# Depth-first stage targets for the planner, taps summed on TensorE, shuffles over alternate partition halves, and weight loads behind the shuffles, in a one-core long convolution with a token MLP

## The chip, the cores and the metric

The kernel runs on one core of a Trainium2 chip. The metric is device time in microseconds, the median of several executions. A core has TensorE (matmuls, results to the PSUM memory of eight banks), VectorE and ScalarE (called DVE and ACT in the profile; both can read PSUM), GpSimd (POOL) and SyncE (SP, which here only issues DMAs). Each engine takes its own instructions strictly in the order in which they stand in its queue.

## The reference, cut to what matters

S = 2048 tokens, D = 448 channels, F = 1792.

```python
def _A_ref(q, k, v, shift_k, ssm_k, ssm_D):
    k_pad = jnp.pad(k, ((0, 0), (ks - 1, 0), (0, 0)))
    k_shift = jnp.zeros_like(k)
    for t in range(ks):                                   # ks = 4 taps
        k_shift = k_shift + k_pad[:, t:t + S, :] * shift_k[:, ks - 1 - t][None, None, :]
    kv = k_shift * v
    ...
    y_f = kv_f * kf_f[None, :, :, :]                      # Fourier transforms of kv and ssm_k, length 2S
    y = irfft2(y_f)[:S]
    y = y + kv * ssm_D[None, None, :]
    return q * y

def _B_ref(x, w1, b1, w2, b2):
    h = _layernorm(x, axis=-1)
    u = jnp.einsum("bsd,sf->bdf", h, w1) + b1
    u = _gelu(u)
    y = jnp.einsum("bdf,fs->bds", u, w2) + b2
    return y.transpose(0, 2, 1)

h = x + _A_ref(_layernorm(x), A_k, A_v, ...)
out = h + _B_ref(_layernorm(h), ...)
```

## The kernel before, in words

A sequence of 2048 is held as 128 partitions of R = 16 consecutive tokens (index r). The convolution is a Fourier transform in two steps of matmuls. **Stage 1** (`emit_stage1`, L863 and L865) multiplies, for each r, the slice by a cosine and a sine table into a pair of PSUM banks; ACT or VectorE evicts the pair (128 x 896, L870) into one of eight buffers (`wring`); GpSimd issues a DMA, the *shuffle* (L873), which spreads the buffer's 128 rows over eight partitions of a tile `T`, sixteen rows each. It runs once for the filter ("k", transposed before by 64 small matmuls in `emit_kT`, L848) and once for kv ("u"). **Stage 2** (`emit_stage2`, L887, evictions L639 to L643) needs all sixteen shuffles of its signal, and gives the spectrum in sixteen slices j of four matmuls. `emit_products_i1` multiplies the two spectra (L916 and L921, VectorE, two products a slice into a ring `mring` of four) and goes back by eight matmuls a slice (L927); the slice is evicted and shuffled again (L933, the *z shuffles*, into `TZ`). `emit_i2` needs all sixteen z shuffles: for each r it sums in one PSUM bank kv times ssm_D (by an identity matmul, L991) and two table matmuls (L993, L995); VectorE multiplies by normalized q (L998) and adds x (L1001), ACT takes mean and square sums (L1004, L1007), GpSimd the power (L1015, L1018), VectorE normalizes (L1023). `emit_mlp` follows: W1 in two parts (W1A, six of the fourteen column blocks, L1057; W1B, eight, L1065), gelu on ACT (L1048), W2 (L1074), and the last addition and store (L1077, L1081).

`emit_kv` makes kv: for each r VectorE multiplies four shifted rows by the four taps (L829, 128 x 1792), for each two r adds them in two steps (L832, L835) and multiplies by v (L838). It uses two buffers T by turns. `emit_ct` reorders the tables on GpSimd (L897) and transposes them (L903). `emit_tables` makes the tables, among them seven block-diagonal ones (`BD`, L751).

The order of each engine's queue is not written by hand. `_Sched.schedule` is a list scheduler that runs at build time: an operation has a planned duration, and among the ready ones an engine takes that of highest priority, the longest planned path to the end plus a `boost`. So slices of equal rank go side by side. Operations given as `FX` may go to ACT or VectorE, whichever the planner finds free. All weight loads are issued from ACT's queue (`WQ = "act"`), and the memory of W1B and W2 is that of the spectra and `TU`, so their issues wait for the last readers of these. Loads of the inputs are issued by SP.

## Time and profile before

| | us |
|---|---|
| median of 3 executions | 250.05 (248.65 to 251.76) |
| the profiled execution | 249.59 |
| its span, first to last instruction | 247.8 |
| TensorE busy | 190.3 (77%) |
| VectorE busy | 130.1 (53%) |
| ACT busy | 105.4 (43%) |
| GpSimd busy | 51.6 (21%) |
| mean granted TensorE clock | 0.900 |

Times in the profile run from the span's start. PE is TensorE, PEld its weight load. "Busy" rows of groups give the sum and the mean of one in ns, then the idle time of the engine just ahead of them and what ended it. The *chain* follows the instruction that ended last backwards, at each step to what it had waited for. The granted clock is 1.00 or 0.50 in this trace, and a matmul of 448 columns takes correspondingly less or more.

### The profile page before, as it was taken

Reading aid. Unit: us, or ns where it says so; the run is one execution under the profiler, and the core shown is the slowest. Engines: PE = TensorE matmul, PEld = TensorE weight load, DVE = VectorE, ACT = ScalarE, POOL = GpSimd, SP = SyncE. Lnnn points to the kernel's source line nnn. Section 1 sums busy time; section 2 is a strip of 40 time slices with the busy share of each in tenths; the row PEclk is TensorE's granted clock in tenths of the full one; section 3 lists DMA queues with packets and bytes.
Section 4 is the critical chain, followed back from the end, with each engine's and each line's share of the span. In section 5 each row is a group of like instructions: output and inputs, shape, how many; then the busy total and the mean of one; then the engine's idle time right before and its main releaser. Section 6 shows DMA issues by size and latency. Waiting matters only on the chain.

```text
span 247.8 us, 2495 instructions
## 1 busy us (share of the span) xinstructions
PE 190.3 (77%) x913; PEld 95.2 (38%) x913; DVE 130.1 (53%) x253; ACT 105.4 (43%) x164; POOL 51.6 (21%) x97
## 2 busy tenths in 40 slices
PE   0375847795959998787380691999999999999992
PEld 0270101132335434333130240455444566777771
DVE  8999999519984999856110499531000000040225
ACT  5759956784643772535110159980222322100000
POOL 3310744535630014423030003430000000000000
PEclk9996775559997999999987599899999999999998
DMA  5999799999970001489999299100000000001023
GB/s 185 282 369 434 215 201 203 192 241 253 240 217 7 0 0 30 122 222 268 233 366 322 65 352 405 79 1 0 3 0 0 0 0 3 0 33 43 2 109 111
DMA packets 15126, 35.97 MB, mean 145 GB/s; under 512 B 3787, under 2 KB 7499, under 8 KB 14986
## 3 DMA queue, kind: packets, MB, share of 16 engines
q0 software_dynamic: 5376, 11.04, 19.5%
q10 hardware_dynamic: 6016, 14.68, 18.9%
q1 hardware_dynamic: 3722, 10.10, 11.5%
q8 instruction: 7, 0.11, 0.2%
q14 instruction: 5, 0.04, 0.1%
HBM read 22.94 MB, written 1.84 MB: 100 GB/s over the span
## 4 chain that ended last, share of the span: by engine, by line
PE 53%; DMA 21%; DVE 11%; ACT 6%; POOL 3%; issue 3%; SPq 1%; DVEq 0%; ACTq 0%; POOLq 0%
DMA arena<-arena 18%; PE ps L1074 17%; PE ps L1065 10%; PE ps L1057 8%; PE ps L887 7%; PE ps L927 7%; ACT arena L639 5%; DMA arena<-in_A_ssm_k_dram 4%; DVE arena L998 3%; POOL arena L873 2%; PE ps L848 2%; DVE arena L1001 2%; DVE arena L954 1%; DVE arena L1077 1%; ACT arena L870 1%
## 5 line engine op out<-in xcount | busy, mean ns | idle before, releaser
L1074 PE MATMUL ps<-arena 128*128 128x448 bf16 x224 | 45.6, 355 | 0.0
L1077 DVE SCALAR_TENSOR_TENSOR arena<-ps,arena 128x448 bf16<-128x448 f32 x16 | 9.7, 676 | 67.4 <-PE ps L1074 67.4
L1074 PEld LDWEIGHTS ps<-arena 128*128 128x128 bf16 x224 | 31.5, 145 | 13.4 <-ACT arena L1048 3.1
L887 PE MATMUL ps<-arena 128*128 128x448 bf16 x128 | 31.2, 386 | 6.8 <-DMA arena<-arena 2.9
L639 ACT CAST arena<-ps 128x896 bf16<-128x896 f32 (+1 forms) x24 | 20.4, 876 | 33.1 <-PE ps L927 18.1
L927 PE MATMUL ps<-arena 128*128 128x448 bf16 x128 | 27.0, 366 | 9.0 <-ACT arena L639 9.0
L1065 PE MATMUL ps<-arena 128*128 128x448 bf16 x128 | 29.4, 353 | 0.0
L870 ACT CAST arena<-ps 128x896 bf16<-128x896 f32 x30 | 25.5, 940 | 6.3 <-DMA arena<-arena 6.3
L1057 PE MATMUL ps<-arena 128*128 128x448 bf16 x96 | 22.6, 372 | 5.2 <-DVE arena L1023 5.2
L1048 ACT ACTIVATE arena<-ps,arena 128x448 bf16<-128x448 f32 x14 | 8.9, 634 | 38.7 <-PE ps L1057 19.4
L873 POOL DMA_DIRECT2D arena<-arena x32 | 19.5, 608 | 25.6 <-ACT arena L870 19.8
L863 PE MATMUL ps<-arena 128*128 128x448 bf16 x32 | 15.1, 471 | 12.3 <-ACT arena L870 7.8
L927 PEld LDWEIGHTS ps<-arena 128*128 128x128 f16 x128 | 12.2, 101 | 23.9 <-ACT arena L639 12.9
L887 PEld LDWEIGHTS ps<-arena 128*128 128x128 f16 x128 | 11.7, 105 | 23.7 <-issue 6.2
L642 DVE CAST arena<-ps 128x896 bf16<-128x896 f32 x9 | 9.6, 1089 | 14.7 <-PE ps L927 9.6
L1065 PEld LDWEIGHTS ps<-arena 128*128 128x128 bf16 x128 | 12.0, 98 | 12.6 <-ACT arena L1048 2.4
L829 DVE TENSOR_TENSOR arena<-arena 128x1792 bf16<-128x1792 bf16 x16 | 16.4, 1079 | 0.0
L1004 ACT ACTIVATE arena<-arena 128x448 bf16<-128x448 bf16 x16 | 9.2, 576 | 15.6 <-PE ps L993 15.2
L1057 PEld LDWEIGHTS ps<-arena 128*128 128x128 bf16 x96 | 9.8, 103 | 15.0 <-DVE arena L1023 5.5
L865 PE MATMUL ps<-arena 128*128 128x448 bf16 x32 | 15.5, 485 | 0.0
L863 PEld LDWEIGHTS ps<-arena 128*128 128x128 f16 x32 | 3.3, 102 | 30.2 <-ACT arena L870 22.9
L998 DVE TENSOR_TENSOR arena<-ps,arena 128x448 bf16<-128x448 f32 x16 | 9.3, 614 | 10.3 <-PE ps L995 10.1
(75 smaller groups left out, 219.0 us busy)
## 6 DMA issues: line engine op xcount, KB each, us to landing
arena<-arena POOLq DMA_DIRECT2D x48, 224.0 KB, 8.3
arena<-in_B_w_dram ACTq DMA_DIRECT2D x5, 2048.0 KB, 12.9
arena<-in_B_w_dram ACTq DMA_DIRECT2D x2, 1536.0 KB, 23.1
arena<-in_A_ssm_k_dram SPq DMA_DIRECT2D x4, 448.0 KB, 7.6
arena<-in_A_k_dram SPq DMA_DIRECT2D x4, 448.0 KB, 12.0
arena<-in_A_v_dram SPq DMA_DIRECT2D x4, 448.0 KB, 12.6
arena<-in_A_q_dram SPq DMA_DIRECT2D x1, 1792.0 KB, 18.1
out_dram<-arena SPq DMA_DIRECT2D x7, 224.0 KB, 1.9
```

Of the source, the lines that this page charges most:

```text
L639: return e.copy(out=dst(), in_=src())
L829: op("dve", lambda e, W, T=T, i=i, r=r: e.tensor_tensor(out=T[:, i], in0=KH[:, r:r + 4, :], in1=WT, op=ALU.mult), r=[(o_KH + r * DB, 4 * D ...
L863: op("pe", lambda e, W, b=b, r=r: e.matmul(Pb(b, 0), Ct[:, r, :], src[:, r, :], start=True, stop=True), r=[r_C(r), (o_src + r * DB, DB)], ...
L865: op("pe", lambda e, W, b=b, r=r: e.matmul(Pb(b, 1), St[:, r, :], src[:, r, :], start=True, stop=True), r=[r_S(r), (o_src + r * DB, DB)], ...
L870: return e.copy(out=dst, in_=Ppair(b)) if W == "act" else e.tensor_copy(out=dst, in_=Ppair(b))
L873: op(SHQ[r % 2], lambda e, W, w=w, p0=p0: e.dma_start(T[p0:p0 + 29:4].rearrange("p j c d -> p j (c d)"), WR(w.slots[0]).rearrange("p c d - ...
L887: op("pe", lambda e, W, b=b, bi=bi, tab=tab, ci=ci, st=st, sp=sp, j=j: e.matmul(Pb(b, bi), tab, T[:, j, ci, :], start=st, stop=sp), r=rr, ...
L927: i = op("pe", lambda e, W, b=b, bi=bi, tab=tab, mi=mi, m=m, k=k: e.matmul(Pb(b, bi), tab, MR(m.slots[0])[:, mi, :], start=(k % 4 == 0), s ...
L998: op("dve", lambda e, W, b=b, r=r: e.tensor_tensor(out=V[:, r, :], in0=Pb(b), in1=Q[:, r, :], op=ALU.mult), r=[(o_Q + r * DB, DB)], w=[(o_ ...
L1057: op("pe", lambda e, W, r=r, fc=fc, b=bs[fc]: e.matmul(Pb(b), W1A[:, r, 128 * fc:128 * fc + 128], Q[:, r, :], start=(r == 0), stop=(r == R ...
L1065: op("pe", lambda e, W, r=r, fc=fc, b=b: e.matmul(Pb(b), W1B[:, r, 128 * (fc - n0):128 * (fc - n0) + 128], Q[:, r, :], start=(r == 0), sto ...
L1074: op("pe", lambda e, W, r=r, fc=fc, b=b: e.matmul(Pb(b), W2[:, fc, r:S:R], G[:, fc, :], start=(fc == 0), stop=(fc == NFC - 1)), r=[(o_W2 + ...
```

## The change

Parts of it move instructions, others replace them.

- **Priorities.** `boost` gives way to `t0`, a target time in us for each operation: a lower target goes first, and the longest path only breaks ties. The targets rise with r, c or j inside a stage, so one slice is finished before the next is begun. Planned durations of VectorE and of DMA issues change, VectorE takes an `FX` operation only when ACT has a backlog of six or is busy for 0.6 us more, and the planner's model of the shuffles puts successive ones on alternate halves of the DMA engines.
- **Taps.** The two additions of `emit_kv` go; for each r four identity matmuls sum the four products in a PSUM bank, and VectorE multiplies the bank by v (128 x 448, sixteen times).
- **kT** is evicted in eight pieces of two r instead of four pieces of four.
- **Shuffles** write other partitions: shuffle r begins at partition 64·(r mod 2) + 32·(r/2 mod 2) + r/4, so successive ones lie in alternate halves of the 128 partitions. The tables (`pc`, `cp`) are permuted to match; GpSimd's four table copies become eight of half the size.
- **i2** adds the identity matmul last instead of first.
- **Weights** are issued by SP; W1A waits for the last u shuffle, W1B and W2 for the last z shuffle. W2 is cut 4, 3, 4, 3 instead of 4, 4, 4, 2.
- The ssm_k loads go ahead of the shift_k load.

```diff
@@ the planner @@
         for o in ops:
-            prio[o.id] += o.boost
+            prio[o.id] = prio[o.id] * 1e-6 - o.t0
...
+                        if (e == "dve" and len(ops[oid].engs) > 1 and
+                                free_at["act"] - t < self.flex_slack and not self.backlog(ready, ops, started, ready_t, t)):
+                            tmp.append((pr, oid))
+                            continue
...
+                        if o.keng == 8:
+                            rr8 ^= 8
+                            use = range(rr8, rr8 + 8)
@@ the targets (two of three lines) @@
+        T_KV, T_DKV, T_KT, T_K1, T_DK1, T_U1, T_DU1 = 12.0, 3.6, 10.0, 14.0, 1.2, 16.0, 2.0
+        T_K2, T_U2, T_D2, T_CT, T_BIAS, T_I1, T_DI1 = 38.0, 56.0, 1.0, 45.0, 50.0, 60.0, 1.6
@@ emit_kv @@
-                op("dve", lambda e, W, T=T: e.tensor_tensor(out=T[:, :, 0:2, :], in0=T[:, :, 0:2, :],
-                                                            in1=T[:, :, 2:4, :], op=ALU.add),
-                   r=[(o, 8 * DB)], w=[(o, 8 * DB)], n=4 * D)
-                op("dve", lambda e, W, T=T: e.tensor_tensor(out=T[:, :, 0, :], in0=T[:, :, 0, :], in1=T[:, :, 1, :],
-                                                            op=ALU.add),
-                   r=[(o, 8 * DB)], w=[(o, 8 * DB)], n=2 * D)
-                op("dve", lambda e, W, T=T, c=c: e.tensor_tensor(out=V[:, 2 * c:2 * c + 2, :], in0=T[:, :, 0, :],
-                                                                 in1=V[:, 2 * c:2 * c + 2, :], op=ALU.mult),
...
+                for i in range(2):
+                    r = 2 * c + i
+                    b = _Buf(psum)
+                    for j in range(4):
+                        op("pe", lambda e, W, b=b, T=T, i=i, j=j: e.matmul(Pb(b), ID, T[:, i, j, :], start=(j == 0),
+                                                                           stop=(j == 3)),
+                           r=[(o_ID, 256), (o + (i * 4 + j) * DB, DB)], bw=[b], n=D)
+                    op("dve", lambda e, W, b=b, r=r: e.tensor_tensor(out=V[:, r, :], in0=Pb(b), in1=V[:, r, :],
+                                                                     op=ALU.mult),
@@ emit_stage1, and the same for the z shuffles with j @@
+                sch.t0 = T_K1 + T_DK1 * r if tag == "k" else T_U1 + T_DU1 * r
...
-                p0 = 32 * (r >> 2) + (r & 3)
-                op(SHQ[r % 2], lambda e, W, w=w, p0=p0: e.dma_start(
+                p0 = 64 * (r & 1) + 32 * ((r >> 1) & 1) + (r >> 2)
+                shuf[tag] = op(SHQ[r % 2], lambda e, W, w=w, p0=p0: e.dma_start(
@@ emit_i2 @@
-                    op("pe", lambda e, W, b=b, r=r: e.matmul(Pb(b), ID, V[:, r, :], start=True, stop=False),
...
+                    k = op("pe", lambda e, W, b=b, r=r: e.matmul(Pb(b), ID, V[:, r, :], start=False, stop=True),
@@ weights @@
-        WQ = "act"
+        WQ = "sp"
...
-                       w=[(o_W1A + 8 * h * 1536, 8 * 1536)], dmab=128 * 8 * 1536)
+                       w=[(o_W1A + 8 * h * 1536, 8 * 1536)], dmab=128 * 8 * 1536, after=[shuf["u"]])
...
-                       w=[(o_W1B + 8 * h * 2048, 8 * 2048)], dmab=128 * 8 * 2048)
+                       w=[(o_W1B + 8 * h * 2048, 8 * 2048)], dmab=128 * 8 * 2048, after=[shuf["z"]])
```

Three places show how the queues change. First TensorE where the inverse stage runs. Before, L927 are its matmuls, eight a slice, and the rows are two slices twice; `csem_act` and `csem_dve` are waits for ACT and VectorE.

```order
L927 MATMUL ps<-arena 128x448 [waits csem_act]
L927 MATMUL ps<-arena 128x448 x4
L927 MATMUL ps<-arena 128x448 [waits csem_act]
L927 MATMUL ps<-arena 128x448 x10
L927 MATMUL ps<-arena 128x448 [waits csem_dve,csem_act]
L927 MATMUL ps<-arena 128x448 x4
L927 MATMUL ps<-arena 128x448 [waits csem_dve,csem_act]
L927 MATMUL ps<-arena 128x448 x10
```

The same stage in the changed order: L953 are the eight matmuls of a slice, L910 the four of stage 2 of a later one.

```order
L910 MATMUL ps<-arena 128x448 [waits csem_act]
L910 MATMUL ps<-arena 128x448 x3
L953 MATMUL ps<-arena 128x448 [waits csem_act,csem_dve]
L953 MATMUL ps<-arena 128x448 x7
L910 MATMUL ps<-arena 128x448 [waits csem_act]
L910 MATMUL ps<-arena 128x448 x3
L953 MATMUL ps<-arena 128x448 [waits csem_act,csem_dve]
L953 MATMUL ps<-arena 128x448 x7
```

Before, sixteen matmuls of two slices were mixed, the second slice begun after five of the first; now a slice is eight in a row, and stage 2 of u runs between.

Second, ACT's queue over the same stretch, before: L639 are evictions, L1039 and L1044 the issues of W1B and W2, L1004 the first statistics of i2.

```order
L639 CAST arena<-ps 128x896 x12
L1039 DMA arena<-in_B_w_dram 128x8x1024
L639 CAST arena<-ps 128x896 x6
L1039 DMA arena<-in_B_w_dram 128x8x1024
L1044 DMA arena<-in_B_w_dram 128x4x2048
L639 CAST arena<-ps 128x896 x2
L1044 DMA arena<-in_B_w_dram 128x4x2048
L1004 ACTIVATE arena<-arena 128x448
```

And in the changed order, from the end of stage 1 (L891) on; L662 are the evictions of k's stage 2, L661 those of u's stage 2 and the inverse stage.

```order
L891 CAST arena<-ps 128x896 x7
L662 ACTIVATE arena<-ps 128x896 x13
L661 CAST arena<-ps 128x896 x31
L1030 ACTIVATE arena<-arena 128x448
L1033 ACTIVATE arena<-arena 128x448
```

The issues have left ACT's queue, and the evictions follow each other.

Third, TensorE in stage 1. Before, stage 1 stands alone, and stage 2 of k (L887) begins while u's stage 1 is under way.

```order
L863 MATMUL ps<-arena 128x448
L865 MATMUL ps<-arena 128x448
L887 MATMUL ps<-arena 128x448 x12
L863 MATMUL ps<-arena 128x448
L865 MATMUL ps<-arena 128x448
```

In the changed order L858 are the tap matmuls, L884 and L886 stage 1, and stage 2 (L910) begins after all of stage 1.

```order
L858 MATMUL ps<-arena 128x448 x4
L884 MATMUL ps<-arena 128x448
L886 MATMUL ps<-arena 128x448
L884 MATMUL ps<-arena 128x448
L886 MATMUL ps<-arena 128x448
...
L910 MATMUL ps<-arena 128x448 x84
```

The taps stand between the stage-1 matmuls, so that a tap waits for whatever the stage-1 matmul ahead of it waits for; and no stage 2 stands inside stage 1.

More of the change, by code (lines that the diff above doesn't have):

```diff
@@ L158, in op @@
         if o.is_dma:
-            o.est = {e: (450.0 if e != "pool" else 1100.0) for e in o.engs}
+            o.est = {e: (600.0 if e != "pool" else 820.0) for e in o.engs}
         elif est is not None:
@@ L235, in est_of, with backlog @@
         return 450.0
+    flex_slack = 600.0
+    flex_back = 6
+    def backlog(self, ready, ops, started, ready_t, t):
+        c = 0
+        for _, i in ready["act"]:
+            if not started[i] and ready_t[i] <= t + 1e-6:
+                c += 1
+        return c >= self.flex_back
     def schedule(self):
@@ L658, in emit_tables @@
             srow = view(o_s, [16], i32)
-            pc = view(o_p, [6], i32)
-            pcf = view(o_p + 24, [4], f32)
+            pc = view(o_p, [8], i32)
+            pcf = view(o_p + 32, [4], f32)
             o_b = small(16)
@@ L847, in emit_kT @@
+        def emit_kT():
+            for g in range(8):
+                sch.t0 = T_KT + 0.9 * g
+                b = _Buf(psum)
+                for rr in range(2):
+                    r = 2 * g + rr
                     for c in range(4):
                         op("pe", lambda e, W, b=b, rr=rr, r=r, c=c: e.transpose(
-                            out=Pbf(b, rr // 2)[:, (rr % 2) * D + 112 * c:(rr % 2) * D + 112 * c + 112],
+                            out=Pbf(b, 0)[:, rr * D + 112 * c:rr * D + 112 * c + 112],
@@ L879, in _build @@
         wbufs = []
+        shuf = {}
         def emit_stage2(T, o_T, scale):
             for j in range(R):
+                sch.t0 = (T_K2 if scale else T_U2) + T_D2 * j
                 b = _Buf(psum, 2)
@@ L894, in emit_ct @@
                 for h in range(2):
+                    sch.t0 = T_CT
                     oc = o_cp + 4096 * k + 2048 * h
                     cp = view(oc, [8, 128], f16)
[L897 to L900 removed]
+                    for z in range(2):
+                        op("pool", lambda e, W, cp=cp, tab=tab, h=h, z=z: e.tensor_copy(
+                            out=cp[:, :, 64 * z:64 * z + 64].rearrange("p r (a f h) -> p r a f h", a=2, f=8),
+                            in_=tab[:, 8 * h:8 * h + 8, :].rearrange("p r (f h a z) -> p r z a f h", f=8, h=4, a=2)[:, :, z]),
+                           r=[(o_tab + 2048 * h, 2048)], w=[(oc, 2048, "cp%d%d" % (k, h))], n=512)
                     b = _Buf(psum)
@@ L1027, in emit_i2 @@
                        kind="4x")
-        WQ = "act"
+        WQ = "sp"
         def emit_w1_load(which):
+            sch.t0 = 60.0 + 40.0 * which
             for h in range(2):
@@ L1085, in emit_mlp @@
                        r=[(o_X + r * DB, DB)], dmab=128 * DB)
+        PLAN = (("tables", emit_tables, ()), ("loads", emit_loads, ()), ("kv", emit_kv, ()), ("kT", emit_kT, ()),
+                ("k1", emit_stage1, (KT, o_KT, TK, o_TK, "k")), ("k2", emit_stage2, (TK, o_TK, 1.0 / 2048.0)),
+                ("u1", emit_stage1, (V, o_V, TU, o_TU, "u")), ("w1a", emit_w1_load, (0,)), ("kvd", emit_kvd, ()),
+                ("ct", emit_ct, ()), ("bias", emit_bias, ()), ("q", emit_q, ()),
+                ("u2", emit_stage2, (TU, o_TU, None)), ("i1", emit_products_i1, ()), ("w1b", emit_w1_load, (1,)),
+                ("i2", emit_i2, ()), ("w2", emit_w2_load, ()), ("mlp", emit_mlp, ()))
         block = ctx.enter_context(nc.Block())
```

136 lines of the change are left out of this document (59 added, 77 removed).

## The prediction, made before the changed kernel had run

> **What bounds the kernel now.** I read the page's clock and DMA rows first, then the windows by stage, then the chain that ended last, then groups and timeline for the price of one instruction. The windows give start:end, then the length, the busy time of each engine, and last the granted TensorE clock, the DMA share and GB/s.
>
> ```profile
> PEclk9996775559997999999987599899999999999998
> DMA  5999799999970001489999299100000000001023
> 0.00:23.00 23.00, 8.89 (x70) 6.33 (x70) 22.01 (x39) 16.06 (x18) 5.76 (x17) 0.95 0.91 310
> 23.00:50.50 27.50, 19.04 (x50) 3.16 (x51) 24.05 (x30) 21.19 (x27) 14.55 (x24) 0.62 0.92 215
> 50.50:74.40 23.90, 17.53 (x85) 7.78 (x85) 18.38 (x40) 13.85 (x16) 10.68 (x18) 0.91 0.96 240
> 74.40:92.00 17.60, 17.19 (x87) 7.60 (x87) 13.50 (x22) 10.99 (x12) 0.00 (x0) 0.90 0.01 2
> 92.00:129.00 37.00, 27.15 (x130) 12.23 (x130) 21.22 (x45) 13.02 (x16) 12.17 (x20) 0.95 0.74 200
> 129.00:138.40 9.40, 0.87 (x4) 0.16 (x4) 0.25 (x1) 0.00 (x0) 1.18 (x2) 0.72 0.91 275
> 138.40:154.00 15.60, 10.34 (x42) 4.68 (x43) 14.49 (x40) 9.43 (x30) 1.27 (x4) 0.83 0.76 282
> 154.00:242.00 88.00, 87.95 (x443) 52.51 (x444) 12.59 (x35) 20.90 (x50) 6.01 (x13) 0.98 0.06 23
> 242.00:247.80 5.80, 1.29 (x7) 0.71 (x5) 3.64 (x6) 0.00 (x0) 0.00 (x0) 0.83 0.32 119
> ...
> 30.50:47.00 16.50, 10.07 (x27) 1.63 (x28) 16.50 (x21) 11.02 (x13) 7.75 (x14) 0.61 1.00 200
> ```
>
> Only the MLP (154 to 242) is full of TensorE. Before it 154 us pass in which no engine is full for long. From 23 to 74.4 stage 1 (k and u) is held by shuffles: the DMA engines are 92 to 100% busy and yet move 200 GB/s, where the loads moved 310. From 92 to 129 the inverse stage takes 37 us for 27 us of TensorE; from 129 to 138.4 all wait for the last z shuffle. The chain says why:
>
> ```profile
> 92.07 3.08 PE ps L927 x15
> ...
> 95.17 0.92 ACT arena L639
> ...
> 96.13 3.03 PE ps L927 x15
> ...
> 113.21 8.96 DMA arena<-arena
> 122.19 0.38 ACTq L1044
> ...
> 122.61 0.92 ACT arena L639
> ...
> 128.89 0.28 issue
> 129.17 0.59 POOL arena L933
> 129.76 8.62 DMA arena<-arena
> ```
>
> Two slices' matmuls run interleaved, so both finish together, and TensorE then waits for an eviction: 4.06 us from 92.07 to 96.13 for two slices. At 113 to 122 ACT, which evicts, stands behind its own W2 load, which waits for a shuffle. The last shuffle needs 8.62 us beside weight traffic.
>
> **The inverse stage, depth first.** In the new order the eight matmuls of a slice stand together, the identity matmuls that held four PSUM banks move behind the z data, and the weight loads leave ACT's queue. So the three waits above go and TensorE is next: VectorE's products (0.62 us each, two a slice, below) and ACT's eviction (0.92) are shorter than eight matmuls. The matmul's pace and the durations that I use:
>
> ```profile
> 160.95 1.14 PE ps L1057 x6
> ...
> 50.50 4.49 PE L887 MATMUL ps<-arena 128*128 128x448 bf16 x12 [0.46 <-ACT arena L870]
> ...
> 23.00 8.24 ACT L870 CAST arena<-ps 128x896 bf16<-128x896 f32 x10
> ...
> 81.13 3.76 ACT L639 COPY arena<-ps 128x1024 f16<-128x1024 f16 x4 [0.27 <-PE ps L903]
> ...
> L916 DVE TENSOR_TENSOR arena<-arena 128x896 bf16<-128x896 bf16 x16 | 9.3, 620 | 6.1 <-PE ps L927 6.0
> L829 DVE TENSOR_TENSOR arena<-arena 128x1792 bf16<-128x1792 bf16 x16 | 16.4, 1079 | 0.0
> L832 DVE TENSOR_TENSOR arena<-arena 128x1792 bf16<-128x1792 bf16 x8 | 8.3, 1080 | 0.0
> L835 DVE TENSOR_TENSOR arena<-arena 128x896 bf16<-128x896 bf16 x8 | 4.6, 612 | 0.0
> L998 DVE TENSOR_TENSOR arena<-ps,arena 128x448 bf16<-128x448 f32 x16 | 9.3, 614 | 10.3 <-PE ps L995 10.1
> ```
>
> A matmul of 448 columns costs 1.14/6 = 0.19 us at full clock and 4.49/12 = 0.374 at half. An eviction of 896 costs ACT 8.24/10 = 0.82 back to back, one of the table transposes 3.76/4 = 0.94. From k's stage 2 to the end of the inverse stage the order has 64 + 64 + 128 = 256 matmuls with nothing else between. ACT has 13 + 31 evictions there, 44 × 0.82 = 36.1 us, and VectorE 32 products, 19.8 us, beside q's statistics: both under TensorE's 256 × 0.19 = **48.6 us**. So I take this stretch as TensorE's.
>
> **Taps on TensorE.** The sums of L832 and L835 go (8.3 + 4.6 us), and L838's multiply by v (4.6 us by L835's row, the same shape) becomes 16 multiplies from PSUM (9.3 us by L998). VectorE's kv part falls from 16.4 + 8.3 + 4.6 + 4.6 = 33.9 to 25.7 us; TensorE gains 64 matmuls, 12.2 to 23.9 us by the clock. The cover of these is TensorE's idle time in stage 1: 23:50.5 has 19.0 busy of 27.5, at a clock of 0.62. Without that cover they cost themselves. VectorE starts kv later, since the block-diagonal tables now wait for ACT's sines, which stand behind the first kT eviction (of the two landing rows here the first is of the k and u shuffles, L873, the second of the z shuffles, L933):
>
> ```profile
> 13.76 1.08 DVE L829 TENSOR_TENSOR arena<-arena 128x1792 bf16<-128x1792 bf16 x1
> ...
> 16.82 6.32 ACT L639 COPY arena<-ps 128x1792 bf16<-128x1792 bf16 x4 [2.51 <-PE ps L848]
> ...
> DMA to landing us min/median/max: 4.3/8.4/13.4
> ...
> 28.29 0.60 POOL arena L873
> 28.88 0.21 issue
> ...
> 64.00 1.07 DVE L870 CAST arena<-ps 128x896 bf16<-128x896 f32 x1
> ...
> DMA to landing us min/median/max: 4.2/7.8/10.0
> ```
>
> I put that delay at 4 us, between 0 and 8.9 (3 ACT lines at most 0.94 and one kT piece, 6.32/4, doubled): kv runs from some 18 to 18 + 25.7 = 44. That is not the last to finish.
>
> **Stage 1.** kT is evicted in eight pieces of 896 instead of four of 1792; seven on ACT by the 0.82 row are 5.7 against 6.32, so I leave ACT's first stage-1 eviction at 23.0, and add the table eviction that now stands behind it (0.94): 23.9. Then ACT has 30 evictions and 3 table evictions: 30 × 0.82 + 3 × 0.94 = 27.4, to 51.4. POOL issues a shuffle each 0.60 + 0.21 = 0.81: 32 in 25.9, as fast as ACT. Two statistics steps between them wait for VectorE; eight ring buffers cover some 3 us of that. The last matmul pair precedes its eviction by two evictions, so k's stage 2 starts at 51.4 - 1.6 = **49.8** (50.5 now, but then with u unfinished until 65).
>
> This needs shuffles every 0.82 us, 224 KB each: 280 GB/s against the 200 of 30.5:47. Two shuffles in flight there wrote the same 64 partitions; now they alternate. The bounds are no gain (200) and the loads' 310; I take the upper, since the engines are 100% busy at 200 GB/s, which looks like two transfers sharing one way in. [...]
>
> **The sum.** k2 starts 49.8; + 48.6 = 98.4 end of the inverse matmuls; + 0.92 eviction + 0.28 = 99.6 issue of the last z shuffle; + 4.2, the shortest landing of a z shuffle above, since W1B and W2 now wait for it: z lands at 103.8 (138.4 now). Then to the MLP: 15.6 now; the MLP matmuls still wait for six free banks, about 13 multiplies, 11 adds and 4 normalizations on VectorE, which I put at 14 (13 × 0.54 + 11 × 0.30 + 4 × 0.35 + 2, by these rows):
>
> ```profile
> 143.03 1.06 DVE arena L998 x2
> 144.09 0.60 DVE arena L1001 x2
> ...
> 153.50 0.70 DVE L1023 TENSOR_SCALAR arena<-arena 128x448 bf16<-128x448 bf16 x2
> ```
>
> So 117.8; + 88.0 MLP + 3 late matmuls (0.6) = 206.4; + 5.8 tail = 212.2 span. The profiled execution took 249.59 with a span of 247.8, so 1.8 more: **214.0 us**. That execution stands 0.2% under the median of 250.05. The loads: W1A goes at some 55, 3.1 MB, needed at 117.8; W1B and W2, 11.5 MB after 103.8, take 41 us at 282 GB/s (the row of 138.4:154, when they ran); W2 is needed 42.6 us after the MLP starts (224 × 0.19), 56.6 after z lands. They are covered at any rate over 203 GB/s. SP, which now issues them, has only the stores behind, which come later. What is late next is TensorE from 50 to 98.
>
> **The rivals.** *Shuffles get no faster* (the change does not do what it says): 229 KB at 200 GB/s is 1.15 us; from the ninth on 24 × (1.15 - 0.82) = 7.9 us: 222. For it: POOL's queue and the eight engines a shuffle are unchanged. *Lock step*: TensorE takes its queue in order, so taps stand behind stage-1 matmuls that wait for ACT, and VectorE waits for taps; stage 1 then ends where it does now (last eviction 64.00 + 1.07) and k2 starts at 64 instead of 49.8: 228. Against it: ACT, the longest, has nothing to wait for but PSUM. *Slower*: the clock stays at half through those 256 matmuls, as in the 12 at 50.50: 256 × (0.374 - 0.19) = 47 us: 261. It decides from 223 matmuls at half clock on (41 us). Against it: 74.4:92 and 92:129 ran at 0.90 and 0.95 with a lighter load.
>
> **How the numbers follow.** Forecast 0.60 (its own range 207 to 221: up to 4 us less if the MLP starts as banks come free and 3 if the early loads help; up to 2.2 more for twelve matmuls at half clock, 5 for waits of POOL and taps). No faster shuffles 0.20, lock step 0.10, better than 207 0.05, slower 0.03, and 0.02 for a stage 1 lost so far that the time comes out the same. 206 to 229 leaves out under 2 in 10. Faster by over 2% (about what a measurement can tell from no change) 0.95, within 0.02, slower 0.03.
>
> **What would show it.** Shuffle-only windows over 280 GB/s; stage-1 evictions without waits for DMA, the last before 53; TensorE over 90% busy at full clock from 50 to 98; the last z shuffle landing in 4 to 5 us near 104; MLP still 88 us. I am wrong if TensorE waits for evictions between 50 and 98, if k2 starts after 56, or if SP's loads end after the MLP needs them.

## The result, and the profile after

| | before | after | forecast |
|---|---|---|---|
| median of 4 executions each, us | 249.35 (247.55 to 251.76) | 208.44 (206.97 to 213.17) | 214.0 (206 to 229) |
| ratio, with 95% interval | | 0.836 (0.827 to 0.845) | |
| the profiled execution / its span | 249.59 / 247.8 | 206.97 / 205.2 | 214.0 / 212.2 |
| k's stage 2 begins | 50.5 | 52.4 | 49.8 |
| last inverse matmul ends | 128 | 101.0 | 98.4 |
| last z shuffle landed | 138.4 | 105.8 | 103.8 |
| MLP begins | 154 | 116.6 | 117.8 |
| last matmul ends | 243.3 | 202.3 | 206.4 |

Single times of one kernel mostly lie within 2 to 3 us of its median (once 4.7); ratios are made from the undisturbed executions, and where only one of six was such (order_old) none is given. "MLP begins" is the time at which the chain passes to the MLP's matmuls; the first of them start up to 1.8 us sooner (at 116.4 in the changed kernel). The page of the changed kernel shows a clock that is full almost throughout; the slice of 5.1 us with the 5 is the wait for the last z shuffle and what follows it.

```profile
PEclk9997999999999999999957999999999999999999
DMA  6999969998859733235649999940000011111111
```

The windows of the changed kernel by its own stages. The columns are start:end, length, busy time of PE, PEld, DVE, ACT and POOL, the granted clock, the DMA share and GB/s.

```profile
0.00:22.00 22.00, 12.49 (x106) 9.57 (x106) 17.72 (x39) 14.80 (x18) 7.25 (x21) 0.92 0.94 322
22.00:52.40 30.40, 25.73 (x121) 9.78 (x119) 27.02 (x42) 27.20 (x34) 18.58 (x32) 1.00 0.87 227
52.40:68.40 16.00, 15.99 (x85) 8.32 (x86) 14.35 (x35) 14.65 (x18) 7.25 (x13) 1.00 0.81 256
68.40:101.00 32.60, 32.60 (x173) 16.65 (x171) 23.65 (x47) 22.90 (x27) 11.32 (x19) 1.00 0.44 117
101.00:105.80 4.80, 0.01 (x1) 0.00 (x0) 0.00 (x0) 0.91 (x1) 0.93 (x2) 0.73 0.51 138
105.80:116.50 10.70, 10.64 (x46) 5.05 (x47) 8.51 (x24) 6.91 (x21) 1.42 (x4) 0.80 0.93 336
116.50:202.30 85.80, 85.77 (x452) 54.12 (x450) 22.50 (x56) 22.62 (x58) 6.05 (x13) 1.00 0.28 113
202.30:205.20 2.90, 0.00 (x0) 0.00 (x0) 0.68 (x1) 0.00 (x0) 0.00 (x0) 1.00 0.12 40
```

From 52.4 to 101.0 TensorE is busy for 48.59 of 48.60 us at full clock. That is the heart of the gain: the same 256 matmuls were spread over 78 us before, from 50.5 to 128. Behind them stand 4.8 us in which nothing but one eviction and the last shuffles runs. Stage 1, from 22 to 52.4, is the longest stretch in which no engine is full; the DMA engines are busy for 87% there and move 227 GB/s.

The chain that ended last in the changed kernel says the same in time order (start, length, what):

```profile
48.44 3.92 DMA arena<-arena
...
52.41 16.06 PE ps L910 x84
...
87.39 13.63 PE ps L953 x72
...
101.05 0.92 ACT arena L661
101.97 0.28 issue
102.25 3.57 DMA arena<-arena
...
105.86 0.55 PE ps L1017
106.42 0.37 PE ps L1019
...
159.93 42.39 PE ps L1106 x224
...
202.34 0.68 DVE arena L1109
```

k's stage 2 waits for the shuffle of k's last slice, then TensorE follows TensorE up to the last inverse slice. The last z shuffle lands 3.57 us after its issue, with no weight load beside it; beside weight loads it took 8.62 before, and 7.29 and 7.17 in w_act and w_sp_nowait.

The end is shorter too. The timeline of the kernel before shows the last matmuls, which end at 239.72 + 3.57 = 243.3, and six last additions in one row that begins at 242.00, where the chain above has one, L1109, of 0.68 us:

```profile
239.72 3.57 PE L1074 MATMUL ps<-arena 128*128 128x448 bf16 x18
...
242.00 3.64 DVE L1077 SCALAR_TENSOR_TENSOR arena<-ps,arena 128x448 bf16<-128x448 f32 x6 [5.14 <-PE ps L1074]
```

The groups of W2 now end one after another, so only the last one's addition and store follow the last matmul: 2.9 us (205.2 - 202.3) instead of 4.5 (247.8 - 243.3). The 242 at which the prediction ended the MLP is the start of that row of additions; seven matmuls still ran behind it (its row 242.00:247.80).

### The profile page after: what moved, and what is told of

It reads as the page before. It is cut to its first block, busy times and chain, and to the rows that moved or that the text cites. A ratio compares the mean times of both kernels' runs of the same rounds, so it can differ in the third digit from the quotient of the medians.

```text
span 205.2 us, 2642 instructions
## 1 busy us (share of the span) xinstructions
PE 183.2 (89%) x977; PEld 103.5 (50%) x977; DVE 114.4 (56%) x241; ACT 110.0 (54%) x174; POOL 52.8 (26%) x101
## 4 chain that ended last, share of the span: by engine, by line
PE 77%; DMA 11%; ACT 7%; DVE 1%; issue 1%; SPq 1%; POOL 1%; ACTq 0%
PE ps L1106 21%; PE ps L910 12%; PE ps L953 12%; PE ps L1096 12%; PE ps L1086 9%; DMA arena<-arena 7%; DMA arena<-in_A_ssm_k_dram 4%; PE ps L858 4%; ACT arena L891 3%; ACT arena L661 2%; PE ps L1017 2%; PE ps L1019 2%; PE ps L1021 2%; PE ps L884 1%; PE ps L886 1%
## 5 line engine op out<-in xcount | busy, mean ns | idle before, releaser
L1109 DVE SCALAR_TENSOR_TENSOR arena<-ps,arena 128x448 bf16<-128x448 f32 x16 | 10.9, 684 | 58.4 <-PE ps L1106 58.4
L1106 PE MATMUL ps<-arena 128*128 128x448 bf16 x224 | 42.5, 352 | 0.0
L1106 PEld LDWEIGHTS ps<-arena 128*128 128x128 bf16 x224 | 32.3, 144 | 10.1
L661 ACT CAST arena<-ps 128x896 bf16<-128x896 f32 (+1 forms) x32 | 26.9, 889 | 10.1 <-PE ps L953 9.7
L891 ACT CAST arena<-ps 128x896 bf16<-128x896 f32 x30 | 25.6, 914 | 3.3 <-DMA arena<-arena 1.9
L910 PE MATMUL ps<-arena 128*128 128x448 bf16 x128 | 25.5, 353 | 0.9 <-DMA arena<-arena 0.9
L953 PE MATMUL ps<-arena 128*128 128x448 bf16 x128 | 25.5, 352 | 0.0
L1096 PE MATMUL ps<-arena 128*128 128x448 bf16 x128 | 25.2, 352 | 0.0
L894 POOL DMA_DIRECT2D arena<-arena x32 | 19.5, 610 | 17.6 <-ACT arena L891 14.4
L1086 PE MATMUL ps<-arena 128*128 128x448 bf16 x96 | 19.5, 353 | 0.0
L1076 ACT ACTIVATE arena<-ps,arena 128x448 bf16<-128x448 f32 x14 | 8.1, 643 | 20.8 <-PE ps L1096 12.8
L910 PEld LDWEIGHTS ps<-arena 128*128 128x128 f16 x128 | 12.4, 98 | 12.8 <-DMA arena<-arena 1.3
L953 PEld LDWEIGHTS ps<-arena 128*128 128x128 f16 x128 | 12.5, 98 | 11.7
L1096 PEld LDWEIGHTS ps<-arena 128*128 128x128 bf16 x128 | 12.5, 98 | 11.7
L858 PE MATMUL ps<-arena 128*128 128x448 bf16 x64 | 16.7, 373 | 0.7 <-ACT arena L891 0.3
L851 DVE TENSOR_TENSOR arena<-arena 128x1792 bf16<-128x1792 bf16 x16 | 17.0, 1080 | 0.0
L959 POOL DMA_DIRECT2D arena<-arena x16 | 9.8, 611 | 25.6 <-ACT arena L661 25.6
L884 PE MATMUL ps<-arena 128*128 128x448 bf16 x32 | 11.3, 358 | 3.3 <-ACT arena L891 3.1
L1086 PEld LDWEIGHTS ps<-arena 128*128 128x128 bf16 x96 | 9.1, 98 | 9.4 <-DVE arena L1024 1.0
L872 PE MATMUL ps<-arena 112*128 112x112 bf16 x64 | 6.9, 299 | 7.2 <-DVE arena L715 4.8
```

Source lines behind the costliest of these rows:

```text
L661: return e.copy(out=dst(), in_=src())
L851: op("dve", lambda e, W, T=T, i=i, r=r: e.tensor_tensor(out=T[:, i], in0=KH[:, r:r + 4, :], in1=WT, op=ALU.mult), r=[(o_KH + r * DB, 4 * D ...
L858: op("pe", lambda e, W, b=b, T=T, i=i, j=j: e.matmul(Pb(b), ID, T[:, i, j, :], start=(j == 0), stop=(j == 3)), r=[(o_ID, 256), (o + (i * 4 ...
L884: op("pe", lambda e, W, b=b, r=r: e.matmul(Pb(b, 0), Ct[:, r, :], src[:, r, :], start=True, stop=True), r=[r_C(r), (o_src + r * DB, DB)], ...
L891: return e.copy(out=dst, in_=Ppair(b)) if W == "act" else e.tensor_copy(out=dst, in_=Ppair(b))
L894: shuf[tag] = op(SHQ[r % 2], lambda e, W, w=w, p0=p0: e.dma_start(T[p0:p0 + 29:4].rearrange("p j c d -> p j (c d)"), WR(w.slots[0]).rearra ...
```

## The experiments

All times of one run are in this table: the median, the ratio to the kernel before from runs on the same chip, and from the profiled execution the milestones. The last four shared one chip, with six executions each. The profiled execution of w_act took 220.35 us, so its milestones belong to a time 2.9 us above its median.

| run | median us | ratio (95%) | k's stage 2 | last z landed | MLP begins | span |
|---|---|---|---|---|---|---|
| changed kernel | 208.44 | 0.836 (0.827 to 0.845) | 52.4 | 105.8 | 116.6 | 205.2 |
| targets_alone | 222.94 | 0.895 (0.890 to 0.900) | 52.0 | 120.8 | 133.4 | 221.3 |
| no_targets | 252.01 | 1.011 (1.003 to 1.019) | 68.0 | 138.7 | 155.6 | 249.1 |
| flat_i1 | 212.72 | 0.857 (0.849 to 0.865) | 52.5 | 109.7 | 121.4 | 209.5 |
| adds_dve | 213.23 | 0.858 (0.852 to 0.863) | 52.6 | 112.4 | 123.4 | 212.0 |
| w_act | 217.50 | 0.874 (0.867 to 0.881) | 58.6 | 117.4 | 130.7 | 218.5 |
| w_sp_nowait | 220.82 | 0.885 (0.875 to 0.895) | 60.7 | 120.0 | 130.4 | 219.0 |
| place_old | 212.26 | 0.854 (0.847 to 0.862) | 54.6 | 110.8 | 121.2 | 209.7 |
| warm | 207.56 | 0.827 (0.820 to 0.835) | 52.1 | 105.5 | 115.8 | 203.3 |
| order_old | 209.99 | none given | 53.5 | 108.7 | 120.1 | 207.6 |
| order_alt | 209.58 | 0.834 (0.828 to 0.841) | 54.8 | 108.2 | 119.7 | 208.9 |
| warm5 | 206.50 | 0.836 (0.832 to 0.840) | 53.1 | 106.4 | 116.8 | 204.3 |
| after5 (changed kernel) | 208.03 | 0.840 (0.835 to 0.845) | 53.1 | 106.5 | 118.0 | 205.5 |

### The targets without the other parts

targets_alone has the new priorities and planner rules; taps, placement, kT and the weights' queue and waits are those of before. The identity matmul last, the new cut of W2 and the earlier ssm_k loads are in it too. Of its edits to the changed kernel the short ones:

```diff
-                p0 = 64 * (r & 1) + 32 * ((r >> 1) & 1) + (r >> 2)
+                p0 = 32 * (r >> 2) + (r & 3)
...
-        WQ = "sp"
+        WQ = "act"
...
-                       w=[(o_W1A + 8 * h * 1536, 8 * 1536)], dmab=128 * 8 * 1536, after=[shuf["u"]])
+                       w=[(o_W1A + 8 * h * 1536, 8 * 1536)], dmab=128 * 8 * 1536)
```

> The kernel before with the targets and the planner's rules alone (and the identity matmul last, and the new cut of W2): the taps on VectorE, the old partitions of the shuffles, kT in four pieces, weights on ACT without the waits. Theory: the order of the inverse stage gives most of the gain (the 37 us of that stage fall to about 29, the last z shuffle's wait of 8 us stays in part), the start of the stages gives nothing: 220 to 230. Rival A: the targets need the other parts, since ACT still stands behind its weight issues and kv still comes late: 235 to 248. Rival B: the targets give all of it: 206 to 212.

Measured: 222.94 us, the theory's case. Of the 41 us between 249.4 and 208.4 the order, with these three small parts, brings 26.5 (249.4 - 222.9). By the milestones: the last z shuffle lands at 120.8 instead of 138.4 (17.6 us), the MLP follows after 12.6 instead of 15.6 (3.0), and MLP and tail take 87.9 instead of 93.8 (5.9). The windows of targets_alone show what it leaves:

```profile
22.00:52.00 30.00, 17.26 (x72) 5.74 (x70) 26.50 (x36) 21.41 (x25) 13.12 (x22) 0.67 0.99 223
...
112.00:120.80 8.80, 0.00 (x0) 0.00 (x0) 0.00 (x0) 0.00 (x0) 0.60 (x1) 0.50 1.05 272
```

Stage 1 still has the DMA engines full and TensorE at a clock of 0.67, and the last z shuffle is still under way for these 8.8 us, beside weights.

### The other parts without the targets

no_targets puts the longest planned path and the boosts back and keeps the rest.

```diff
-            prio[o.id] = prio[o.id] * 1e-6 - o.t0
+            prio[o.id] += BOOST(o)
```

> The changed kernel with the old priorities (longest planned path and boost) and everything else kept: taps on TensorE, alternate halves, weights on SP behind the shuffles, new planned durations. In this order all 64 tap matmuls stand ahead of the first stage-1 matmul on TensorE. Theory: the taps then wait for VectorE until some 47 us and stage 1 starts only after that, 27 us (32 evictions) later stage 2 starts: near 74 instead of 52.4; then 256 matmuls at some 0.25 us with the mixed slices; 235 to 250, so the targets carry the gain and the other parts without them give little. Rival A: the taps, the placement and the weights carry most of it, and the order of slices matters little: 212 to 225. Rival B: worse than the kernel before, over 255, since the taps lock TensorE and VectorE together.

Measured: 252.01 us, 1.1% over the kernel before, between the theory's 250 and rival B's 255. The first row of its windows is the stretch of the taps, the second the inverse stage:

```profile
16.00:40.00 24.00, 18.63 (x91) 8.83 (x91) 23.77 (x33) 8.78 (x13) 0.00 (x0) 0.93 0.34 140
...
95.70:133.00 37.30, 28.04 (x128) 12.89 (x126) 15.34 (x27) 13.15 (x16) 8.95 (x15) 0.91 0.29 76
```

From 16 to 40 VectorE is full with kv, TensorE works off taps, and GpSimd issues no shuffle at all: the 64 taps stand ahead of stage 1 in TensorE's queue. Stage 2 begins at 68.0, 15.6 us later than in the changed kernel. The inverse stage takes 37.3 us again, as before the change (37.0), although the weight issues have left ACT. So the other parts are worth 14.5 us with the targets (222.9 - 208.4) and lose 2.6 without them; and the 37 us of that stage come back with the old priorities alone. How much of that is the rank of the slices, the next run asks.

### Only the inverse stage's slices back to equal rank

```diff
-        T_K2, T_U2, T_D2, T_CT, T_BIAS, T_I1, T_DI1 = 38.0, 56.0, 1.0, 45.0, 50.0, 60.0, 1.6
+        T_K2, T_U2, T_D2, T_CT, T_BIAS, T_I1, T_DI1 = 38.0, 56.0, 1.0, 45.0, 50.0, 60.0, 0.0
```

> The changed kernel with one target for all sixteen slices of the inverse stage (the step of 1.6 us per slice set to 0), so that slices of equal rank go side by side again in part of that stage; all else as changed. Theory: a slice's eight matmuls no longer end ahead of the next one's, TensorE waits for evictions and PSUM banks between groups, up to the 4 us per two slices that the trace of before shows, for those slices that are mixed: the inverse matmuls end at 104 to 112 instead of 101.0 and the time is 211 to 219. Rival: ACT's 0.92 us against 1.5 us of TensorE a slice leaves so much room that mixing costs nothing once the weight issues have left ACT: 207 to 210, TensorE at over 97% from 52 to 101.

Measured: 212.72 us, 4.3 more, in the theory's range. In its queue the first slice still stands alone, and most later ones are mixed, up to four together. The chain of this run has the mixing as the old trace had it, matmuls of four slices in a row and then a wait for an eviction, only rarer:

```profile
72.36 5.50 PE ps L953 x29
77.86 0.02 issue
77.88 0.92 ACT arena L661
78.80 0.05 issue
78.84 1.74 PE ps L910 x8
80.58 5.55 PE ps L953 x29
86.14 0.02 issue
86.16 0.92 ACT arena L661
```

Its inverse matmuls end at 103.7 instead of 101.0, 0.3 under the theory's lower end; the rest is that evictions and shuffles now come in bunches, so the last shuffle lands 6.0 us behind the last matmul (4.8 in the changed kernel). So equal ranks in this one stage cost 4.3 us in the changed kernel. The larger part of the 26.5 must then come from the other targets, with which stage 2 of u still runs between the inverse slices; no run parts them.

### Taps back on VectorE

```diff
-                    for j in range(4):
-                        op("pe", lambda e, W, b=b, T=T, i=i, j=j: e.matmul(Pb(b), ID, T[:, i, j, :], start=(j == 0),
-                                                                           stop=(j == 3)),
...
+                op("dve", lambda e, W, T=T: e.tensor_tensor(out=T[:, :, 0:2, :], in0=T[:, :, 0:2, :],
+                                                            in1=T[:, :, 2:4, :], op=ALU.add),
```

> The changed kernel with the taps summed by VectorE in two additions and one multiply as before; all else as changed. Theory: kv takes VectorE 33.9 us instead of 25.7, so the last kv slice comes 8 us later, at some 55 instead of 47.6; u's stage 1 then ends near 60, but k's stage 2 (64 matmuls, 12 us) can run meanwhile, so only what is left counts: u's stage 2 starts at 60 + 4 instead of 52.4 + 12.2 = 64.6. So 0 to 4 us more, 208 to 213. Rival A: VectorE is the one that decides and the whole 8.2 us come back: 216 to 218. Rival B: the tap matmuls in stage 1 were a burden on TensorE, and without them the time falls: 204 to 207.

Measured: 213.23 us, 4.8 more: 0.2 over the theory's upper end and below rival A. k's stage 2 begins on time (52.6), but the last shuffle of u is issued at 65.3 instead of 54.7, and the end of the inverse matmuls slips to 107.7. Rival B is out: the taps are no burden. The same stretch in adds_dve:

```profile
22.00:52.50 30.50, 18.40 (x52) 3.21 (x51) 30.50 (x42) 25.12 (x31) 16.16 (x27) 0.72 0.83 218
```

The changed kernel's row of 22.00:52.40 stands above: 121 matmuls in 25.73 us at a clock of 1.00. Here 52 take 18.40 us at 0.72. The 69 more matmuls cost 7.3 us of busy time, 0.11 each, less than the 0.19 of one at full clock: the granted clock was 1.00 with them and 0.72 without. And VectorE, full here (30.50 of 30.50), gets room. How the 4.8 us divide between the two, no run shows.

### Weights: the queue, and the waits

w_act issues them from ACT with no wait for shuffles; w_sp_nowait lacks the waits too, but leaves the issues with SP, without the first two lines of this diff.

```diff
-        WQ = "sp"
+        WQ = "act"
...
-                       w=[(o_W1A + 8 * h * 1536, 8 * 1536)], dmab=128 * 8 * 1536, after=[shuf["u"]])
+                       w=[(o_W1A + 8 * h * 1536, 8 * 1536)], dmab=128 * 8 * 1536)
```

> The changed kernel with the loads of W1 and W2 issued from ACT's queue as before and with no wait for shuffles; all else as changed. Theory: ACT stands behind issues whose memory is not free and the last z shuffles meet weight traffic: z lands 8 us after its issue instead of 3.6, and ACT loses some 4 us at one issue; part of that is given back since weights come earlier, which nobody waits for. 213 to 220. Rival A: the depth-first order alone removed those waits, the queue does not matter: 207 to 210. Rival B: W1A in the middle of stage 1 takes the DMA engines from the shuffles for 3.1 MB at 390 GB/s = 8 us, TensorE's start at 52.4 slips by all of it, and the z end slips too: 220 to 226.

> The changed kernel with the weights still issued by SP, but without the added waits for the last u and z shuffles (they still wait for their memory to be free); all else as changed. It parts the two halves of the run with the loads on ACT: here ACT never stands behind an issue, and only the traffic beside the shuffles differs from the changed kernel. Theory: W1A's 3.1 MB run beside stage 1 and W1B and W2 beside the last z shuffles, as their memory comes free: z lands 6 to 8 us after its issue instead of 3.6, k's stage 2 starts 0 to 4 us later; 211 to 216. Rival: the waits are redundant, because the memory comes free only then: 207 to 210 and the same landing of the last z shuffle.

Measured: 217.50 and 220.82 us, 9.1 and 12.4 more. w_act falls into its theory's range, but not by the theory's sum: k's stage 2 starts 6.2 us later there, as only rival B had it, and the z shuffle takes 3.7 us more. w_sp_nowait goes past its theory's 216. The windows of the last z shuffle in w_act, in w_sp_nowait and in the changed kernel, one after another:

```profile
110.10:117.40 7.30, 0.00 (x0) 0.00 (x0) 0.00 (x0) 0.00 (x0) 0.57 (x1) 0.71 1.03 406
```

```profile
112.90:120.00 7.10, 0.00 (x0) 0.00 (x0) 0.00 (x0) 0.00 (x0) 0.55 (x1) 0.76 1.04 404
```

```profile
102.30:105.80 3.50, 0.00 (x0) 0.00 (x0) 0.00 (x0) 0.00 (x0) 0.55 (x1) 0.63 0.45 125
```

The engines are full with weights in the first two (DMA shares of 1.03 and 1.04 against 0.45), and the shuffle needs twice as long, 7.29 and 7.17 us against 3.57, whichever queue issued them. The start of k's stage 2 has the same cause. In w_sp_nowait SP issues W1A at 39.6 and 45.3, in the middle of stage 1, and the chain has k's last shuffle behind it:

```profile
49.60 11.03 DMA arena<-arena
...
60.67 19.54 PE ps L910 x90
```

11.03 us against 3.92, at a DMA share of 1.04 and 308 GB/s from 49.6 to 60.6. ACT, further behind in its queue, issued W1A only at 48.0 and 53.1, and lost less (7.38, k's stage 2 at 58.6). So on SP's queue the waits are worth 12.4 us, and without them SP's freedom does harm, 3.3 us more than ACT's queue. What the queue is worth with the waits stays open, since no run has them on ACT. ACT's own price shows behind z: 13.3 us from landing to MLP (117.4 to 130.7) against 10.7, as its i2 statistics stand behind two issues of W2.

### Placement of the shuffles

place_old puts the old first partitions back, with the tables that go with them; GpSimd then makes four copies of tables instead of eight, and the planner orders the rest differently.

```diff
-                p0 = 64 * (r & 1) + 32 * ((r >> 1) & 1) + (r >> 2)
+                p0 = 32 * (r >> 2) + (r & 3)
```

> The changed kernel with every shuffle on the partitions that it had before (and the tables' order that goes with them); all else as changed. Theory: two successive shuffles in one half share a way in, so stage 1 is held by 200 GB/s instead of 232. 24 shuffles of 229 KB cost 24 x (1.15 - 0.99) = 3.9 us more, k's stage 2 starts at 55 to 58 instead of 52.4, and the time is 212 to 215 against 208.4. Rival A: the placement does nothing, ACT's evictions or GpSimd's issues set the pace: 208, k's stage 2 at 52.4, the rate in stage 1 within 5% of 232 GB/s. Rival B: all of the 2.6 us by which the prediction missed the start of k's stage 2 and more hang on it, since the buffers run empty: over 218.

Measured: 212.26 us, 3.8 more, and so it seemed the theory's case; but its rate from 30 to 47 was 232 GB/s, the changed kernel's, as rival A had it, and u's last stage-1 matmuls stood at 63.2 in its chain, inside stage 2. That is the planner's other order, so this run can't settle the placement. order_old is therefore the changed kernel with the old partitions in the access patterns alone, every queue word for word the same, and order_alt the opposite, strict alternation in the order of issue (the tables stay, so both compute other numbers). This is order_alt's line:

```diff
-                p0 = 64 * (r & 1) + 32 * ((r >> 1) & 1) + (r >> 2)
+                p0 = {"k": (0, 64, 96, 1, 32, 97, 65, 33, 2, 34, 98, 66, 99, 3, 35, 67),
+                      "u": (32, 64, 0, 96, 65, 1, 33, 66, 2, 97, 34, 67, 3, 98, 35, 99)}[tag][r]
```

> The changed kernel, instruction for instruction in the same order, with the old first partition of each shuffle in its access pattern and nothing else (the tables keep the new order, so the numbers that it computes are other ones). In that order k and u shuffles are mixed, and by the old numbering 0 to 12 of the 32 fall nearly all in the lower half, the next ten are mixed and the last nine in the upper half. Theory: shuffles that write one half share a way in and stay at 200 to 207 GB/s, mixed ones reach 240 to 258, so 21 of 32 shuffles take up to 1.15 us instead of 0.99: k's stage 2 starts 1 to 3.4 us later than 52.4, the last z shuffles do not change much, and the time is 1 to 4 us over the changed kernel. Rival: the placement does nothing, and the 200 GB/s of before came from eight shuffles in flight; then the times agree within 0.5 us and k's stage 2 starts at 52 to 52.8.

> The changed kernel, instruction for instruction in the same order, with first partitions chosen so that the 32 shuffles of stage 1 alternate between the halves in the order in which GpSimd issues them, k and u together (in the changed kernel each signal alternates by itself, and where k and u are mixed neighbours fall into one half ten times of 31). The tables keep their order, so the numbers that it computes are other ones. Theory: strict alternation gives little, since some six are in flight and both halves are about equally filled already: within 1 us of the changed kernel, the rate from 30 to 47 us at 225 to 245 GB/s. Rival: neighbours in one half are what holds the rate at 232; then it nears 280 to 310 there, k's stage 2 starts at 50 to 51.5 and the time falls by 1 to 2.5 us.

> The changed kernel again, as the yardstick of the three others on this chip. Every theory expects 207.5 to 209.5, k's stage 2 at 52 to 53 and the MLP at 116 to 117.

Measured: medians 209.99 (206.32 to 212.43) for order_old, 209.58 (205.44 to 210.74) for order_alt, 208.03 (206.25 to 209.44) for the changed kernel. Two microseconds at most, inside the scatter. The windows of order_old first, then of after5:

```profile
30.00:38.00 8.00, 5.66 (x24) 2.05 (x23) 5.90 (x8) 5.72 (x8) 4.50 (x8) 0.90 0.98 200
38.00:42.00 4.00, 3.68 (x15) 1.31 (x13) 3.08 (x5) 3.47 (x5) 1.80 (x4) 0.78 1.02 239
```

```profile
30.00:38.00 8.00, 6.67 (x32) 2.40 (x31) 7.30 (x11) 6.79 (x8) 4.94 (x10) 1.00 0.94 239
38.00:42.00 4.00, 2.39 (x12) 0.81 (x10) 2.91 (x5) 3.04 (x4) 1.81 (x4) 1.00 1.02 220
```

From 30 to 38 nearly all of order_old's shuffles, k's and u's, go to the lower half: 200 GB/s with the engines full, the very rate of the kernel before. At 38 to 42 k has gone to the upper half and u not: 239. In the changed kernel 239 is there from the start, though it falls to 220 from 38 to 42. So with every queue the same the placement does change the rate, by 20% in the first window and by 7% from 30 to 47 (213 against 229 GB/s), and the rival, in which it does nothing, is out. That sharing one half is the reason is not shown, for strict alternation, in order_alt, gives hardly more than one half alone:

```profile
30.00:38.00 8.00, 4.89 (x22) 1.56 (x21) 6.84 (x9) 5.41 (x7) 3.98 (x7) 1.00 0.90 209
```

Its DMA engines were not even full (a share of 0.90). Its theory was right in that it gains nothing, but expected 225 to 245 GB/s from 30 to 47, where it moved 208; the cause stays open. The time hardly knows of any of this: stage 1 of order_old lets k's stage 2 begin at 53.5, against 52.4 and 53.1 in the changed kernel.

### Matmuls into the idle gap

```diff
+            for i in range(24):
+                k = op("pe", lambda e, W, b=b, i=i: e.matmul(Pb(b), ID, V[:, 0, :], start=(i == 0), stop=(i == 23)),
+                       r=[(o_ID, 256), (o_V, DB)], bw=[b], n=D, after=[i1_last[-1]] if i == 0 else ())
```

> The changed kernel with 24 more matmuls, whose result nobody reads, between the last matmul of the inverse stage and the first of the last stage of the convolution, so that TensorE is not idle in the 4.8 us for which it waits for the last z shuffle. Theory: the granted clock stays at 1.00 and the twelve matmuls at 0.37 us that follow the gap (105.9 to 110.1) run at 0.19: up to 12 x 0.18 = 2.2 us less, of which VectorE's multiply and the six banks leave 0.5 to 1.5; 207 to 208 against 208.4, the MLP start at 115 to 116. Rival A: VectorE sets the pace there, no change in time though the clock is full. Rival B: the clock falls all the same.

> The changed kernel with the 24 idle-time matmuls again, beside the changed kernel itself on the same chip. Theory: about 1 us under it, since the clock no longer falls to half for the first twelve matmuls behind the last z shuffle and VectorE then sets the start of the MLP (115.8 against 116.6) ; ratio to the changed kernel 0.993 to 0.998. Rival: no difference, the earlier 207.6 against 208.4 was scatter.

Measured: 207.56 against 208.44, then 206.50 against 208.03 on one chip. The stretch from the landed z shuffle to the MLP in warm5, then in after5:

```profile
106.40:116.80 10.40, 10.22 (x53) 4.78 (x53) 9.55 (x27) 7.68 (x23) 1.91 (x4) 1.00 0.90 332
```

```profile
106.50:118.00 11.50, 11.40 (x52) 5.19 (x53) 9.62 (x27) 7.70 (x23) 1.91 (x4) 0.88 0.93 340
```

The clock stays at 1.00, as the theory had it, and the MLP begins 1.2 us earlier (116.8 against 118.0). In both of these runs VectorE ends last before the MLP; it starts its last stretch 1.2 us sooner in warm5, because the matmul that it waits for ends 1.2 us sooner. The chain of warm5, then that of after5:

```profile
111.58 0.61 DVE arena L1034
...
116.77 2.14 PE ps L1096 x10
```

```profile
112.77 0.61 DVE arena L1024
...
117.96 2.14 PE ps L1086 x10
```

In the changed kernel's first profile TensorE ended last: its chain has the matmuls behind the gap at half clock from 105.86 to 110.14, 4.3 us. The half clock behind the gap did not last equally long everywhere: 4.3 us here after 4.8 idle, 2.8 in after5 (106.54 to 109.34) after 4.8 too, and 6.2 in w_act (117.40 to 123.56) after 8.6. Both comparisons went the same way, but the intervals of the two ratios overlap (0.832 to 0.840 and 0.835 to 0.845): probably the best version here, by some 1.5 us, and not settled.

## Why the prediction was right, step by step

The forecast was 214.0 and the profiled execution took 206.97. The steps, against the span of 212.2 that was forecast (205.2 measured, 7.0 less):

- *k's stage 2 at 49.8*: 52.4, 2.6 late, and the one step that came out worse. The term at fault is the shuffles at 280 GB/s, for which I took the upper bound, 310, over the lower, 200. Measured in the changed kernel, in the window of stage 1 in which shuffles alone run, and what ACT's 30 evictions waited for (us, times), from the list of its line L891:

```profile
30.00:47.00 17.00, 14.27 (x69) 5.85 (x69) 14.91 (x23) 14.54 (x18) 9.65 (x18) 1.00 0.97 232
```

```profile
DMA arena<-arena: 3.0, 5
PE ps L886: 1.3, 2
```

232 GB/s, so the engines stay full and ACT waited five times for a buffer, where the prediction left it nothing to wait for but PSUM. Its stage-1 evictions began 1.6 us earlier than planned (22.25 against 23.9) and k's stage 2 still began only at 52.4. A second thing was missing in the step: k's stage 2 needs the landing of k's last shuffle, 3.92 us behind its issue, and I had it start when the matmuls of stage 1 were through; 0.85 us of the 2.6 are TensorE idle for that.
- *The pairs of halves*: the direction was right and the size too great. The reason ("two transfers sharing one way in") fits order_old, 200 against 239 GB/s in the same order of issue, and does not fit order_alt's 209, so it is not shown. Neither the 239 nor the 209 comes near the 310 of the loads. The first rival (222) needed a stage 1 that hangs on the rate; order_old, 2.0 us over the changed kernel and inside the scatter, shows that it hangs on it by no more than some 2 us.
- *256 matmuls in 48.6 us, TensorE alone*: 48.6 (52.41 to 101.0), to the tenth. The three waits of the trace of before are gone, and flat_i1 brings part of the first back and costs 4.3 us. The slow rival, half clock, did not come: 1.00 throughout.
- *Eviction, issue and a last z shuffle of 4.2 us*: 0.92 + 0.28 + 3.57. That it needs the added waits was argued from one fast row; w_act and w_sp_nowait show it, 7.3 and 7.2 us without.
- *14 us from z to the MLP*: 10.7. The six banks come free while VectorE is still at work on other slices; I had summed VectorE's multiplies, additions and normalizations and added 2. In this profile TensorE, not VectorE, sets the stretch (10.64 of 10.70 us busy, VectorE 8.51); in after5 VectorE ends last and it takes 11.5. The range had up to 4 us less as a possibility.
- *MLP 88.6 and tail 5.8, unchanged*: 85.8 and 2.9. I had read the end of the MLP as 242, where seven matmuls (1.29 us) were still to come. By the true end, 243.3, the MLP went from 89.3 to 85.7 us and the tail from 4.5 to 2.9. In the MLP the clock accounts for some 1.5 us, an estimate: before, the 7.0 us from 154 on ran at a granted clock of 0.78, now at 1.00. The other 2 us are open. In the tail I had overlooked that the targets also end W2's groups one after another.
- *Loads covered*: so they were; the MLP has no wait for DMA in the chain.
- *Taps free under TensorE's idle time*: right, and more than free, see adds_dve. *Lock step* did not come with the targets; without them (no_targets) it did, and k's stage 2 began 15.6 us later.

So +2.6, -0.6 (z landing), -3.3, -2.8 and -2.9 make the -7.0. The main mechanism of the forecast, a stretch that is TensorE's alone, held. Its sizes erred in both directions, so it is partly luck that the sum came out only 3% high. Of the signs that it named, two did not come: windows of shuffles alone over 280 GB/s, and stage-1 evictions without waits for DMA.

Not tried: the identity matmul last, kT in eight pieces, the cut of W2 and the order of the ssm_k loads, each by itself, and the waits with ACT's queue; and no run parts the 1.75 us of k's late start that evictions' waits explain between DMA and the order of the taps in TensorE's queue.

## What to carry to other kernels

When engines wait for each other in turns and none is full, look first at the order of equal work: two slices mixed mean that both end late. A target time for every slice and stage was worth more here (26.5 us, with three small parts in it) than the other parts of the change, which without that order lost 2.6; the ranks inside the inverse stage alone were worth 4.3 in the changed kernel. Bulk loads that nobody waits for yet should be held back by a wait until the small transfers that somebody does wait for have landed; the waits made 12.4 us here. And a part of a change that moves a measured rate by 20% may move the time by less than the scatter, so test it with every queue kept as it is.

## What the runs showed of the hardware that I had not expected

- The granted clock was 0.72 with 52 matmuls from 22 to 52.5 us (adds_dve), 0.67 with 72 from 22 to 52 (targets_alone), and 1.00 with 121 from 22 to 52.4 (changed kernel). After 4.8 us of idleness eleven matmuls ran at half clock, ten of them at 0.37 us instead of 0.19 (105.9 to 110.1 in the changed kernel; seven, to 109.3, in after5); with 24 matmuls in the gap it stayed at 1.00 (warm5, 101.7 to 116.8).
- From 30 to 38 us, shuffles nearly all to one half of the partitions kept the DMA engines full (a share of 0.98) at 200 GB/s (order_old). Each signal alternating between the halves gave 239 there (after5), strict alternation of both together 209 (order_alt), and weights and the last z shuffle together moved 404 to 406 (w_sp_nowait, w_act). The last z shuffle lands in 3.6 us without weights beside it, and beside weights in 7.2 to 7.3 (w_sp_nowait, w_act).
